# Second half of the sink values loaded in the second batch, the first batch's shifted values copied on VectorE, and a plan with measured first arrivals

## The chip, the cores and the metric

The kernel runs on one core of a Trainium2 chip. The metric is the time of one execution in microseconds (us) on the device, the median of several runs. The engines are TensorE (PE in the profile; PEld are its weight loads), VectorE (DVE), ScalarE (ACT), GpSimd (POOL) and SyncE (SP). POOL issues the large loads of q, k and the weights, SP the loads of v and the stores.

## What is computed

Four batches of attention with 8 heads of 64 over 768 positions, then a mixing layer on the result. Three heads attend to everything before them. The five others ("stream" heads) see the first 4 positions, the sinks, and a window of 64. Cut to what matters:

```python
stream_keep = causal & (is_sink | in_win)        # n_sink = 4, window = 64
a = softmax(where(mask, q @ k.T / 8, -1e9))
x = (a @ v) as [batch, 768, 512]
theta = x @ w_theta
y = w_tok_r @ (x * cos(theta)) + w_tok_i @ (x * sin(theta))
u = x + y
out = u + relu(u @ w_ch)
```

## The kernel before

Every batch goes through the same steps. PE transposes q and k, two heads (a pair) at a time (`turn_qk`, L251), and ACT or DVE copies the result out (`keep_qk`, L258 and L260, tiles `qT`, `kT`). PE multiplies scores into `ps` (L322), ACT takes the exponent into `P` (full heads) or `P_st` (stream heads), POOL cuts `P` at the diagonal (L200) and DVE multiplies `P_st` by the window's mask (L358). `sink_scores` (L385) and `sink_exps` (L389) make the weights of the sinks, `p_sink`. Then `values` (L409) multiplies the weights by v, one row block of 128 positions at a time, `normalize` divides by the sums (L414, L416) into `x`, and `turn_x`, `theta` (L432), `wave` (L437 and L439, `ct` and `st`), `z_real` (L442, DVE) and `z_imag` (L445, POOL, in the first batch partly DVE) prepare the mixing: `mix` (L455, `py`), `make_u` (L459), `channel` (L474) and `finish` (L478). The token weights `wtok` are loaded by POOL (L487), transposed on PE (L494) and copied out by ACT or DVE (L498).

Three copies of v are needed. `vt` holds v in bf16 (`cast_v`, L222). `vx` holds it shifted by 64 positions for the stream heads (`shift_v`: L228 and L229 from `vt` in the first batch, L232 and L233 from the loaded tile later). `vs` holds the sinks' values of all batches: `sink_values` (L244) loads the 4 sink positions of two batches into a small tile `vs_f`, which DVE casts into `vs` (L698). `vs_f` is one buffer, and both halves go through it: batches 0 and 1, then 2 and 3.

In the first batch the loads of v (`load_v`, L218, eight DMAs from SP into the four buffers `st_v`) are held back by a small DVE write that depends on the first transposed k (L216).

All steps are put into a `Plan`. Each has an engine, an estimated duration, the steps that it follows and the buffers that it takes. `Plan.order` runs a list scheduler over these estimates, and the code is emitted in the order of the planned starts. So the estimates set the order of instructions on each engine; what an engine really waits for is set by the data. Buffers also tie engines together: `ps`, `pav` and the theta tiles share two PSUM buffers (pool `s`), the transposes share two others (`x`). The plan's `gate` says when the first loads of q and k arrive, and in it one engine "DMA" carries all transfers, one after the other.

Of the kernel before, what the change touches and what calls it, by code (L numbers as in the profile page):

```python
# [31 lines left out]
class Plan:  # L32
# [3 lines left out]

    LATENCY = {"PE": (230, 0), "ACT": (190, 60), "DVE": (120, 60), "POOL": (150, 60), "SP": (50, 0), "DMA": (2000, 0)}
    SWITCH = {"PE": 95, "ACT": 1300}  # L40
    HOLD = {"PE": 1500, "ACT": 8000}

# [11 lines left out]
    def order(self, free):  # L54
# [26 lines left out]
        while events:  # L81
            now = events[0][0]
            while events and events[0][0] <= now:
                _, _, done = heapq.heappop(events)
                if done is not None:
                    for g in done.give:
                        holding[id(g)] -= 1
                        if holding[id(g)] == 0:
                            slots[g.take] += 1
            for e in engines:  # L90
                if free.get(e, 0) > now:
                    continue
                best = None
                for s in ready.get(e, ()):
                    if ready_at[id(s)] > now or (s.take and slots[s.take] < 1):
                        continue
                    value = -ready_at[id(s)] if e == "DMA" else rank[id(s)] + s.bias
                    if s.mode and s.mode != mode.get(e):
                        value -= self.HOLD.get(e, 0)
                    if best is None or value > best[0]:  # L100
                        best = (value, s)
                if best is None:
                    continue
                s = best[1]
                ready[e].remove(s)
                t = now
                if s.mode and s.mode != mode.get(e):
                    if mode.get(e):
                        t += self.SWITCH.get(e, 0)
                    mode[e] = s.mode  # L110
                if s.take:
                    slots[s.take] -= 1
                s.start, s.end = t, t + s.ns
                out.append(s)
                lat = self.LATENCY[e]
                free[e] = s.end
                heapq.heappush(events, (s.end, count, None))
                heapq.heappush(events, (s.end + lat[0], count + 1, s))
                heapq.heappush(events, (s.end + lat[1], count + 2, None))
                count += 3  # L120
                for n in later[id(s)]:
# [12 lines left out]
def kernel(  # L134
# [14 lines left out]
    nc = tc.nc  # L149
# [393 lines left out]

    cleared = [add(eng, ns, lambda n=n: clear(n)) for n, (eng, ns) in enumerate((("DVE", 900), ("POOL", 1300), ("DVE", 600), ("POOL", 1300)))]
    landed = {}
    gate = [add("DMA", ns, None) for ns in (2600, 2400, 4800)]
    for n in range(4):
        for what in "qk":
            landed[what, 0, n] = gate[min(n, 2)]
# [36 lines left out]
    def v_steps(b):  # L586
        for n in range(4):
            if b == 0:
                issue = add("DVE", 200, lambda n=n: load_v(0, n, kT[n // 2]), [kept["k", 0, n // 2]], take="st_v")
                land = add("DMA", 2000, None, [issue])  # L590
            else:
                issue = add("SP", 1500, lambda b=b, n=n: load_v(b, n), [cast[b - 1, n], xk[b - 1, 5]], take="st_v")
                land = add("DMA", 2000, None, [issue])
            old = [s for key, s in av.items() if key[0] == b - 1] if b else [cleared[1]]
            cast[b, n] = add("DVE" if b == 0 else "POOL", 570 if b == 0 else 830, lambda b=b, n=n: cast_v(nc.gpsimd if b else nc.vector, b, n), [land] + old, give=[issue])
            for x, h in enumerate(PAIRS[n]):
                if not IS_RETR[h]:
                    shift[b, h] = add("POOL", 960, lambda b=b, n=n, x=x: shift_v(nc.gpsimd, b, n, x), [cast[b, n]], give=[issue])

    def attention_steps(b):  # L600
        got = {}
# [56 lines left out]
    def mlp_steps(b):  # L658
        for t in range(NB):
# [6 lines left out]
            ch[b, t] = add("PE", 864, lambda b=b, t=t: channel(b, t), [uk, channel_w], take="m", give=[uk], mode="128")  # L666
            fin = add("DVE", 680, lambda b=b, t=t: finish(b, t), [ch[b, t]], take="ot", give=[ch[b, t], ud[b, t]], bias=URGE)
            st = add("SP", 100, lambda b=b, t=t: store(b, t), [fin])
            add("DMA", 900, None, [st], give=[fin])

    turn_steps(0)
    v_steps(0)
# [19 lines left out]
    weights(4, 2, [])  # L692
    ones_done = add("POOL", 600, sink_ones, [cleared[3]])
    sink_done = []
    for half in range(2):
        first = add("SP", 500, lambda half=half: sink_values(2 * half), [cleared[2]] + sink_done)
        land = add("DMA", 100, None, [first])
        sink_done.append(add("DVE", 480, lambda half=half: nc.vector.tensor_copy(vs[:32, 2 * half:2 * half + 2, :, :D], vs_f), [land, cleared[3], ones_done]))  # L698
# [54 lines left out]
```

## Time and profile before

| what | us |
|---|---|
| median of 3 runs | 226.41 (226.37, 226.41, 229.37) |
| the profiled execution, its own time | 229.25 |
| its span, first to last instruction | 227.5 |
| busy: PE, PEld | 195.2, 113.1 |
| busy: DVE, ACT, POOL | 122.2, 120.2, 101.1 |

The profiled execution is 2.84 us longer than the median, and 1.75 us of its own time lie outside the span. PE is busy for 86% of the span, the other engines for 44% to 54%: the time is that of PE's work and of the places at which PE waits. Times of single instructions below are from the span's start.

### The profile page before, as it was taken

To read this page: it belongs to the slowest core of one execution; us is meant where nothing else is said; L and a number is where in the kernel's file an instruction comes from. 1 tells how busy PE (TensorE), PEld (TensorE's weight loads), DVE (VectorE), ACT (ScalarE), POOL (GpSimd) and SP (SyncE) were. 2 spreads that over 40 slices of the span, in tenths; PEclk is the share of its full clock that TensorE was granted. 3 is DMA by queue.
4 is the path that set the end of the run, shared out by engine and by line. 5 is a ranking of instruction groups with operands and counts; after the bars stand their busy time and mean duration, and the time that the engine had idled before them with its cause. 6 is when DMAs were issued, how large, how long until landed. Compare 5 with 4: busy or idle time off the path is not lost.

```text
span 227.5 us, 5040 instructions
## 1 busy us (share of the span) xinstructions
PE 195.2 (86%) x2124; PEld 113.1 (50%) x2124; DVE 122.2 (54%) x203; ACT 120.2 (53%) x156; POOL 101.1 (44%) x180
## 2 busy tenths in 40 slices
PE   0688549968997899999999999959999999689990
PEld 0555339634554577544553468525544575234440
DVE  6327815389542168479135168495451764974341
ACT  2477402793499960184777563644977526703120
POOL 7955992072488300349852200299835000780000
PEclk9999999999999589999999999997999999999997
DMA  6994599999994934902103000960012000210303
GB/s 76 164 210 108 80 174 213 192 200 199 195 209 98 202 55 118 208 14 81 49 0 127 14 0 3 242 178 0 3 48 94 3 3 0 92 49 0 138 0 140
DMA packets 39759, 22.63 MB, mean 99 GB/s; under 512 B 25912, under 2 KB 36664, under 8 KB 39736
## 3 DMA queue, kind: packets, MB, share of 16 engines
q0 software_dynamic: 11072, 9.70, 27.4%
q1 hardware_dynamic: 28664, 12.61, 21.2%
q8 instruction: 16, 0.26, 0.5%
q14 instruction: 7, 0.06, 0.1%
HBM read 25.71 MB, written 6.29 MB: 141 GB/s over the span
## 4 chain that ended last, share of the span: by engine, by line
PE 72%; DVE 8%; ACT 6%; DMA 5%; POOL 3%; issue 3%; POOLq 1%; SPq 1%; DVEq 0%; ACTq 0%
PE py L455 26%; PE pav L409 9%; PE ps L322 9%; PE pc L474 7%; PE pt L251 7%; PE ps L432 6%; DVE zr L442 5%; POOL zi L445 3%; PE pt L421 3%; PE pt L464 3%; DMA vs_f<-in_v_dram 2%; PE pt L494 2%; DMA kb<-in_k_dram 2%; ACT P L341 2%; ACT P_st L338 1%
## 5 line engine op out<-in xcount | busy, mean ns | idle before, releaser
L455 PE MATMUL py<-zr,wtokTr 128*128 128x512 bf16 x144 | 39.7, 385 | 6.3 <-DVE zr L442 6.3
L445 POOL TENSOR_TENSOR zi<-x,st 128x512 bf16<-128x512 bf16 x20 | 27.8, 1421 | 25.2 <-ACT st L439 19.8
L455 PE MATMUL py<-zi,wtokTi 128*128 128x512 bf16 x144 | 38.5, 379 | 0.1
L459 DVE TENSOR_TENSOR u<-x,py 128x512 bf16<-128x512 bf16 x24 | 16.5, 687 | 36.1 <-PE py L455 36.1
L322 PE MATMUL ps<-qT,kT 64*64 64x128 bf16 (+6 forms) x380 | 26.7, 266 | 6.5 <-ACT P L341 2.2
L442 DVE TENSOR_TENSOR zr<-x,ct 128x512 bf16<-128x512 bf16 x24 | 27.9, 1197 | 1.3 <-ACT ct L437 1.3
L468 ACT COPY uT<-pt 128x512 bf16<-128x512 bf16 x24 | 13.9, 586 | 26.5 <-PE pt L464 26.4
L478 DVE SCALAR_TENSOR_TENSOR ot<-pc,u 128x512 f32<-128x512 f32 x24 | 16.5, 688 | 16.4 <-PE pc L474 15.1
L222 POOL CAST vt<-st_v 128x768 bf16<-128x768 f32 x12 | 10.2, 856 | 33.3 <-DMA st_v<-in_v_dram 33.1
L322 PEld LDWEIGHTS <-kT 64*64 64x64 bf16 (+1 forms) x380 | 13.6, 113 | 21.7 <-issue 17.1
L200 POOL TENSOR_SCALAR_AFFINE_SELECT P<-P 128x256 bf16<-128x256 bf16 (+1 forms) x48 | 16.5, 365 | 17.2 <-ACT P L346 6.6
L474 PE MATMUL pc<-w_ch_sb,uT 128*128 128x512 bf16 x96 | 24.0, 380 | 0.0
L432 PE MATMUL ps<-w_theta_sb,xT 128*128 128x512 bf16 x96 | 23.2, 379 | 0.9 <-ACT st L439 0.9
L437 ACT ACTIVATE ct<-ps,half_pi 128x1024 f32<-128x1024 f32 x12 | 13.0, 1113 | 20.1 <-PE ps L432 19.5
L341 ACT ACTIVATE P<-ps 128x1024 bf16<-128x1024 f32 (+2 forms) x24 | 21.2, 923 | 4.5 <-PE ps L322 4.5
L455 PEld LDWEIGHTS <-wtokTr 128*128 128x128 bf16 x144 | 12.6, 98 | 19.7 <-issue 7.6
L258 ACT COPY qT<-pt 128x768 bf16<-128x768 bf16 x14 | 11.0, 802 | 18.7 <-PE pt L251 18.5
L455 PEld LDWEIGHTS <-wtokTi 128*128 128x128 bf16 x144 | 13.3, 98 | 14.9 <-issue 0.4
L358 DVE TENSOR_TENSOR P_st<-P_st,m_stream 128x512 bf16<-128x512 bf16 (+2 forms) x24 | 12.8, 543 | 14.7 <-ACT P_st L349 10.5
L409 PE MATMUL pav<-vx,P_st 128*128 128x65 bf16 x120 | 17.4, 207 | 3.5 <-POOL vx L228 3.5
L409 PE MATMUL pav<-vt,P 128*128 128x65 bf16 x252 | 16.1, 207 | 1.8 <-DVE x L416 1.8
L409 PE MATMUL pav<-vt,P_st 128*128 128x65 bf16 x120 | 17.5, 208 | 0.0
(73 smaller groups left out, 323.8 us busy)
## 6 DMA issues: line engine op xcount, KB each, us to landing
st_v<-in_v_dram SPq DMA_DIRECT2D x32, 192.0 KB
out_dram<-ot SPq DMA_DIRECT2D x24, 256.0 KB
qb<-in_q_dram POOLq DMA_DIRECT2D x3, 768.0 KB, 10.8
kb<-in_k_dram POOLq DMA_DIRECT2D x3, 768.0 KB, 15.4
wtok<-in_moe_w_tok_r_dram POOLq DMA_DIRECT2D x3, 384.0 KB, 11.9
wtok<-in_moe_w_tok_i_dram POOLq DMA_DIRECT2D x3, 384.0 KB, 12.7
w_theta_sb<-in_moe_w_theta_dram POOLq DMA_DIRECT2D x1, 512.0 KB, 5.7
w_ch_sb<-in_moe_w_ch_dram POOLq DMA_DIRECT2D x1, 512.0 KB, 21.1
```

The source lines that it names most:

```text
L200: nc.gpsimd.affine_select(out=t, in_=t, compare_op=ALU.is_ge, fill=0.0, base=base, pattern=pattern, channel_multiplier=cm)
L251: nc.tensor.transpose(pt[64 * x:64 * x + 64, j * 128:(j + 1) * 128], state[what, b][:, h, j * D:(j + 1) * D], ident)
L322: nc.tensor.matmul(ps[half, yy, c:c + w], l, r, start=True, stop=True, skip_group_check=True)
L341: nc.scalar.activation(P.rearrange("p (y c) -> p y c", y=2), ps[:, :, :w0], AF.Exp, scale=scale)
L409: nc.tensor.matmul(o, l, r, start=(m == 0), stop=True, skip_group_check=True)
L432: nc.tensor.matmul(ps[:, y], state["xT", b][:, kk, (i + y) * 128:(i + y + 1) * 128], w_theta_sb[:, kk], start=(kk == 0), stop=(kk == KD - 1))
L442: nc.vector.tensor_tensor(state["zr", b][:, i + y], state["x", b][:, i + y], state["ct", b, i][:, y], ALU.mult)
L445: (nc.vector if eng == "DVE" else nc.gpsimd).tensor_tensor(state["zi", b][:, i + y], state["x", b][:, i + y], state["st", b, i][:, y], ALU ...
L455: nc.tensor.matmul(py, wtokT[n][:, s, t * 128:(t + 1) * 128], z[:, s], start=(g == 0 and m == 0), stop=(g == 2 and m == 3))
L459: nc.vector.tensor_tensor(u, state["x", b][:, t], state.pop(("py", b, t)), ALU.add)
L474: nc.tensor.matmul(pc, uT[:, kk], w_ch_sb[:, kk], start=(kk == 0), stop=(kk == KD - 1))
L478: nc.vector.scalar_tensor_tensor(ot, state.pop(("pc", b, t)), 0.0, state.pop(("u", b, t)), ALU.max, ALU.add)
```

## The change

Three parts. The second half of the sink values (`sink_values(2)` and its cast) moves from the first batch into the second (`sink_steps(1, ...)`, after `v_steps(1)`). In the first batch the shifted copies `vx` are made on DVE, not on POOL. And the plan's estimates change: the first arrivals in `gate`, the time of a v load's issue on SP, and a second planned transfer engine "DMAH" for the DMAs that SP issues. The estimates alter no instruction, but the whole order is planned anew from them, in all four batches.

```diff
-    gate = [add("DMA", ns, None) for ns in (2600, 2400, 4800)]
+    gate = [add("DMA", ns, None) for ns in (4300, 2000, 6000)]
...
-                land = add("DMA", 2000, None, [issue])
+                land = add("DMAH", 2000, None, [issue])
             else:
-                issue = add("SP", 1500, lambda b=b, n=n: load_v(b, n), [cast[b - 1, n], xk[b - 1, 5]], take="st_v")
-                land = add("DMA", 2000, None, [issue])
+                issue = add("SP", 700, lambda b=b, n=n: load_v(b, n), [cast[b - 1, n], xk[b - 1, 5]], take="st_v")
+                land = add("DMAH", 2000, None, [issue])
...
-                    shift[b, h] = add("POOL", 960, lambda b=b, n=n, x=x: shift_v(nc.gpsimd, b, n, x), [cast[b, n]], give=[issue])
+                    shift[b, h] = add("POOL" if b else "DVE", 960 if b else 340, lambda b=b, n=n, x=x: shift_v(nc.gpsimd if b else nc.vector, b, n, x), [cast[b, n]], give=[issue])
...
-            add("DMA", 900, None, [st], give=[fin])
+            add("DMAH", 900, None, [st], give=[fin])
...
-    for half in range(2):
-        first = add("SP", 500, lambda half=half: sink_values(2 * half), [cleared[2]] + sink_done)
-        land = add("DMA", 100, None, [first])
-        sink_done.append(add("DVE", 480, lambda half=half: nc.vector.tensor_copy(vs[:32, 2 * half:2 * half + 2, :, :D], vs_f), [land, cleared[3], ones_done]))
+    def sink_steps(half, after):
+        first = add("SP", 1500, lambda: sink_values(2 * half), [cleared[2]] + after)
+        land = add("DMAH", 300, None, [first])
+        sink_done.append(add("DVE", 480, lambda: nc.vector.tensor_copy(vs[:32, 2 * half:2 * half + 2, :, :D], vs_f), [land, cleared[3], ones_done]))
+
+    sink_steps(0, [])
     attention_steps(0)
     for b in range(1, B):
         turn_steps(b)
         v_steps(b)
+        if b == 1:
+            sink_steps(1, [sink_done[0], cast[1, 0]])
```

The order on DVE in the first batch, from the loads of v to the first row of values: before, from the second cast of v to the division of row 0 (L414, L416).

```order
L222 CAST vt<-st_v 128x2x6x64
L358 TENSOR_TENSOR P_st<-P_st,m_stream 128x2x8x64
L222 CAST vt<-st_v 128x2x6x64
L358 TENSOR_TENSOR P_st<-P_st,m_stream 128x2x8x64
L358 TENSOR_TENSOR P_st<-P_st,m_stream 128x8x64
L698 CAST vs<-vs_f 32x10x64
L222 CAST vt<-st_v 128x2x6x64
L358 TENSOR_TENSOR P_st<-P_st,m_stream 128x2x4x64 x2
L358 TENSOR_TENSOR P_st<-P_st,m_stream 128x4x64
L698 CAST vs<-vs_f 32x10x64
L414 RECIPROCAL r<-pav 128x8
L416 TENSOR_TENSOR x<-pav,r 128x2x4x64
```

The second `L698` stands directly ahead of the first division. The same engine in the changed kernel, from the first cast of v (it follows the two copies `kT_92` and `kT_93` of the first two pairs):

```order
L222 CAST vt<-st_v 128x2x6x64
L698 CAST vs<-vs_f 32x10x64
L228 COPY vx<-vt 64x390
L229 COPY vx<-vt 64x325
L358 TENSOR_TENSOR P_st<-P_st,m_stream 128x8x64
L222 CAST vt<-st_v 128x2x6x64
L260 COPY qT_90<-pt 128x768
L260 COPY kT_94<-pt 128x768
L222 CAST vt<-st_v 128x2x6x64
L260 COPY qT_91<-pt 128x768
L260 COPY kT_95<-pt 128x768
L222 CAST vt<-st_v 128x2x6x64
```

The first cast of v, the one remaining sink cast and the first shifted copy now stand ahead of the copies of the third and fourth pair (`qT_90` to `kT_95`), which they followed before. From there to the first division:

```order
L358 TENSOR_TENSOR P_st<-P_st,m_stream 128x2x8x64
L228 COPY vx<-vt 64x390
L229 COPY vx<-vt 64x325
L228 COPY vx<-vt 64x390
L229 COPY vx<-vt 64x325
L358 TENSOR_TENSOR P_st<-P_st,m_stream 128x2x8x64
L228 COPY vx<-vt 64x390
L229 COPY vx<-vt 64x325
L228 COPY vx<-vt 64x390
L229 COPY vx<-vt 64x325
L358 TENSOR_TENSOR P_st<-P_st,m_stream 128x2x4x64 x2
L358 TENSOR_TENSOR P_st<-P_st,m_stream 128x4x64
```

Four more shifted copies stand between the masks, and no sink cast is left ahead of the division, which follows. On SP, before:

```order
L244 DMA vs_f<-in_v_dram 4x2x64 x5
L218 DMA st_v<-in_v_dram 128x6x64 x8
L244 DMA vs_f<-in_v_dram 4x2x64 x5
L218 DMA st_v<-in_v_dram 128x6x64 x8
L481 DMA out_dram<-ot 128x512 x3
```

And in the changed kernel:

```order
L244 DMA vs_f<-in_v_dram 4x2x64 x5
L218 DMA st_v<-in_v_dram 128x6x64 x16
L244 DMA vs_f<-in_v_dram 4x2x64 x5
L481 DMA out_dram<-ot 128x512 x3
L218 DMA st_v<-in_v_dram 128x6x64 x8
```

The second batch's eight v loads moved ahead of the second sink load. On POOL, at the end of the first batch and the start of the second, before:

```order
L487 DMA wtok<-in_moe_w_tok_r_dram 128x2x768
L487 DMA wtok<-in_moe_w_tok_i_dram 128x2x768
L208 DMA qb<-in_q_dram 128x8x384
L445 TENSOR_TENSOR zi<-x,st 128x512 x2
L208 DMA kb<-in_k_dram 128x8x384
L240 COPY kS_97<-kT_94 64x4 x2
L240 COPY kS_98<-kT_95 64x4 x2
L222 CAST vt<-st_v 128x2x6x64
L232 CAST vx<-st_v 64x6x64
L233 CAST vx<-st_v 64x5x64
```

And in the changed kernel:

```order
L487 DMA wtok<-in_moe_w_tok_r_dram 128x2x768
L445 TENSOR_TENSOR zi<-x,st 128x512 x2
L222 CAST vt<-st_v 128x2x6x64
L487 DMA wtok<-in_moe_w_tok_i_dram 128x2x768
L222 CAST vt<-st_v 128x2x6x64 x2
L232 CAST vx<-st_v 64x6x64
L233 CAST vx<-st_v 64x5x64
L232 CAST vx<-st_v 64x6x64
L233 CAST vx<-st_v 64x5x64
L232 CAST vx<-st_v 64x6x64
L233 CAST vx<-st_v 64x5x64
L240 COPY kS_97<-kT_94 64x4 x2
```

The second batch's casts of v now follow the two `zi` at once, ahead of the small sink keys `kS`; the loads of q and k for the third batch come later. On DVE at that place the order before is one `L498`, four `zr` (L442), one `L498`, two `zi`, two `zr`, two `zi`; in the changed kernel it is four `zr`, two `zi`, two `L498`, two `zr`, two `zi`. On PE the row blocks of values in the first batch came in the order 0, 5, 2, 1, 4, 3 and come now in the order 0, 2, 1, 4, 5, 3; the six transposes of a token weight that stood among them (L494) now stand behind the first products with `w_theta`.

More of the change, by code (lines that the diff above doesn't have):

```diff
@@ L32 @@
 class Plan:
-    LATENCY = {"PE": (230, 0), "ACT": (190, 60), "DVE": (120, 60), "POOL": (150, 60), "SP": (50, 0), "DMA": (2000, 0)}
+    LATENCY = {"PE": (230, 0), "ACT": (190, 60), "DVE": (120, 60), "POOL": (150, 60), "SP": (50, 0), "DMA": (2000, 0), "DMAH": (2000, 0)}
     SWITCH = {"PE": 95, "ACT": 1300}
@@ L96, in order @@
                         continue
-                    value = -ready_at[id(s)] if e == "DMA" else rank[id(s)] + s.bias
+                    value = -ready_at[id(s)] if e[:3] == "DMA" else rank[id(s)] + s.bias
                     if s.mode and s.mode != mode.get(e):
```

## The prediction

> **What bounds the kernel now.** I read the busy shares first, then PE's own waits, then the chain of work that ended last, then the timelines of the first 60 us. PE is busy for 86% of the span, so time is won where PE waits. Of PE's waits (us in total, times, longest) one stands in this change's reach by itself:
>
> ```profile
> PE pav L409 <- POOL vx L228: 3.5, 3, 1.5
> ```
>
> The first batch's value rows wait 3.5 us for POOL's shifted copies. The chain (start, us, what) shows what comes behind:
>
> ```profile
> 25.71 0.68 DVE vs L698
> 27.75 5.37 DMA vs_f<-in_v_dram
> 33.19 0.51 DVE vs L698
> 33.85 0.70 DVE x L416
> 34.60 1.50 PE pav L409 x24
> 36.10 0.43 PE pt L421 x4
> 36.52 0.64 PE pt L494 x6
> 37.16 2.81 PE pav L409 x51
> 39.97 0.72 PE pt L421 x8
> 40.69 0.84 PE pav L409 x27
> 41.76 0.86 PE ps L432 x4
> ```
>
> `vs_f` is one tile, so its second load follows the first cast. DVE takes its work in order and waits for that load with the division behind it, and the third value row, which needs a `ps` buffer back, starts only at 34.60. The reader is also to see a pace: 51 value products take 2.81 us (55 ns each) up to 39.97, 27 take 0.84 (31 ns) after it. PE runs at half pace until it has worked without a break for about 5.8 us from 34.60, to 40.4.
>
> **First part: the start of the first batch.** The changed order puts the first cast of v ahead of DVE's copies of pairs 2 and 3, so the arrival of v is a new wait, and with it come late `qT` and `kT`, for which PE's scores wait. Of the eight pieces of 192 KB that SP asks for, the hardware queue had moved from 8 us on, up to 16, to 20 and to 21.5 us (packets, MB, share):
>
> ```profile
> q1 hardware_dynamic: 2755, 0.69, 38.8%
> q1 hardware_dynamic: 5859, 1.47, 54.7%
> q1 hardware_dynamic: 6272, 1.57, 52.0%
> st_v<-in_v_dram SPq DMA_DIRECT2D x32, 192.0 KB
> ```
>
> That is 3.6, 7.7 and all eight pieces. They are asked for in order, so I take the first pair's two as there by 16.0, the second's soon after and the third's by 20. The prices on DVE, what DVE did at 16, and what POOL gives up:
>
> ```profile
> L260 DVE COPY kT<-pt 128x768 bf16<-128x768 bf16 x10 | 9.2, 949 | 4.5 <-PE pt L251 4.5
> L358 DVE TENSOR_TENSOR P_st<-P_st,m_stream 128x1024 bf16<-128x1024 bf16 x8 | 6.3, 783 | 3.8 <-ACT P_st L338 3.6
> L358 DVE TENSOR_TENSOR P_st<-P_st,m_stream 128x512 bf16<-128x512 bf16 x12 | 5.2, 443 | 0.9 <-ACT P_st L349 0.5 <-ACT P_st L338 0.4
> ...
> L222 DVE CAST vt<-st_v 128x768 bf16<-128x768 f32 x4 | 2.6, 639 | 0.0
> ...
> L228 POOL COPY vx<-vt 64x390 bf16<-64x390 bf16 x5 | 3.1, 619 | 1.6 <-DVE vt L222 1.5
> ```
>
> ```profile
> 15.96 0.96 DVE L260 COPY qT<-pt 128x768 bf16<-128x768 bf16 x1 [4.05 <-PE pt L251]
> 33.63 0.18 DVE L414 RECIPROCAL r<-pav 128x8 f32<-128x8 f32 x1
> ```
>
> DVE was idle for 4.05 us before 15.96, so the wait to 16.0 costs nothing; what stands between it and `qT` does. No row shows a shifted copy on DVE. Above stands twice POOL's 0.62 for the larger of the two pieces, 1.2 us; below, half of what DVE's cast gives for 390 + 325 of its 768 elements (0.639 x 715 / 768 = 0.59), since it reads half the bytes: 0.3. I take 0.5 for both, nearest to DVE's own cast.
>
> From 16.0 DVE then does a cast 0.64, the sink cast 0.6 (between its 0.68 and 0.51), `vx` 0.5, a mask 0.44 and a cast 0.64: 18.8. Then `qT` and `kT` (0.95 each): 20.7; a cast, `qT`, `kT`: 23.3. What PE did at these points before:
>
> ```profile
> 20.52 0.85 PE L322 MATMUL ps<-qT,kT 64*64 64x128 bf16 x26
> 22.29 0.92 PE L322 MATMUL ps<-qT,kT 64*64 64x128 bf16 x26 [0.92 <-ACT P_st L338]
> 24.06 0.40 PE L322 MATMUL ps<-qT,kT 64*128 64x256 bf16 x2 [0.85 <-ACT P_st L338]
> 24.55 1.76 PE L385 MATMUL ps<-qT,kS 128*128 128x512 bf16 x6
> ```
>
> PE reached pair 2 at 20.52 by its own work, so 20.7 costs 0.2. Pair 3 waits for 23.3, 1.0 later. The two products at 24.06 with their 0.85 of waiting now stand earlier in the order, so the sink scores start about 0.35 later than 24.55 and end at 26.7. On DVE a cast, a mask of 0.78, two `vx`, a mask of 0.78 and two `vx` follow 23.3 and end at 27.5; then the last shifted copy is there, and row 0 is done at 27.8. Row 2 takes 24 x 0.055 = 1.3, to 29.1. Three small masks (0.44, 0.44 and under that) end at about 28.75, the division (0.18 + 0.70) at 29.65, a buffer is free, and the third value row starts at 29.7 against 34.60: 4.9 earlier.
>
> From there PE has four rows of 21 + 30 + 33 + 27 = 111 products and 16 transposes (0.43, 0.43, 0.72) before theta: at half pace 6.2 + 1.6 = 7.75, to 37.45. If full pace comes 5.8 us after 29.7 again, at 35.5, the last 1.95 shrink by half and theta starts at 36.5, where before it started at 41.6 (a little ahead of the chain's 41.76). **Term: -5.1 us.** Its bounds are -4.1 (half pace throughout) and -6.3 (the first rival). The loads keep up: on SP the second batch's v is asked for right behind the first's, and on POOL, rid of `vx`, `w_theta` and the token weights come earlier too.
>
> **Second part: theta to the first mixing.** This stage hangs on theta and moves with it, but its order changed on DVE, POOL and ACT (the last two rows are ACT's and PE's):
>
> ```profile
> 46.84 5.39 DVE L442 TENSOR_TENSOR zr<-x,ct 128x512 bf16<-128x512 bf16 x4
> 52.62 1.28 DVE L445 TENSOR_TENSOR zi<-x,st 128x512 bf16<-128x512 bf16 x2
> 48.64 3.59 DVE L442 TENSOR_TENSOR zr<-x,ct 128x512 bf16<-128x512 bf16 x1
> 49.38 2.29 POOL L445 TENSOR_TENSOR zi<-x,st 128x512 bf16<-128x512 bf16 x2
> 147.98 4.21 DVE L442 TENSOR_TENSOR zr<-x,ct 128x512 bf16<-128x512 bf16 x3
> 49.09 0.82 ACT L498 COPY wtokTr<-pt 128x768 bf16<-128x768 bf16 x1
> 52.28 2.10 PE py L455 x9
> ```
>
> A `zr` or `zi` takes DVE 0.64 (half of 1.28) when POOL is idle. The fourth `zr` took 3.59: it ended after both of POOL's `zi` were through. A load issue that stood ahead of those `zi` on POOL is gone, so the fourth `zr` may now pass first: up to 2.9 won on DVE. But POOL casts the second batch's v right behind its two `zi`, so the six `zi` and `zr` that ran alone before run beside it. Where POOL was busy throughout, three `zr` took 4.21, 1.4 each or 0.75 more than alone: 6 x 0.75 = 4.5 lost. PE's own limit is that the transposes of the imaginary token weight now wait for two ACT copies behind `st` (49.09 and 2 x 0.82, then two transposes of 0.2 to 0.25): `py` starts at 51.2 or later in this stage's old time, 1.1 ahead of 52.28 at best. Worse than taking turns is that one of DVE's waits spans POOL's whole queue:
>
> ```profile
> L222 POOL CAST vt<-st_v 128x768 bf16<-128x768 f32 x12 | 10.2, 856 | 33.3 <-DMA st_v<-in_v_dram 33.1
> L232 POOL CAST vx<-st_v 64x384 bf16<-64x384 f32 x15 | 8.0, 534 | 0.4
> L233 POOL CAST vx<-st_v 64x320 bf16<-64x320 f32 x15 | 7.2, 480 | 0.7
> ```
>
> Three casts and six shifted pieces are 3 x 0.86 + 3 x 1.01 = 5.6. The ends are thus -1.1 and 5.6 - 2.9 = +2.7; taking turns gives 4.5 - 2.9 = +1.6. I take **+0.5**, between the better end and taking turns, which a row shows.
>
> The rule of the Trainium skill (SBUF — State Buffer, "Who interferes with whom") is that a DVE instruction with two SBUF inputs and a POOL instruction that reads SBUF exclude each other for one whole instruction. By it each of the six waits for one POOL instruction at most, and the term ends at taking turns, +1.6. The 3.59 row agrees that they exclude each other, but its wait spanned two, so I leave the end at +2.7.
>
> **The rest.** The second sink cast costs 0.51 on DVE, now behind the third `u`. It lies where DVE had nothing to do, up to the third `u`'s row and after it:
>
> ```profile
> 63.33 0.69 DVE L459 TENSOR_TENSOR u<-x,py 128x512 bf16<-128x512 bf16 x1 [3.59 <-PE py L455]
> ```
>
> Without that cover it would cost its 0.5. Its five small DMAs stand on SP behind the v loads and ahead of the first store, and nothing waits for them in the first batch. The new estimates also reorder batches 2 and 3; the same instructions run there, I can read no gain or loss from their order, and take 0 with 1.5 to either side.
>
> **Sum.** -5.1 + 0.5 = -4.6 us. The terms come from the profiled execution of 229.25 us (span 227.5), 2.84 longer than the median of 226.41; they lie in stages that every execution has, so I take them from the median: 226.4 - 4.6 = 221.8 us.
>
> **Rivals.** First, more is won: full pace comes 3.4 us after 29.7, at 33.1, theta starts at 35.3 (-6.3), and the stage's better end adds -1.1: 219.0. For it: 5.8 us is a single observation. Against it: it is the only one. The Trainium skill (TensorE: Matmul & The Clock Gate, "What's actually happening") states that a free-running window of 3.4 us, once busy, opens PE's clock; by that rule the opening lies between 33.1 and 36.5 here, -6.3 to -4.6. The trace's 5.8 us agree with it.
>
> Second, DVE bounds the first 30 us: a pair's shifted copy costs 1.2 us as on POOL. The five are 3.5 more, and so is theta's start: -1.6 + 0.5, 225.3. For it: POOL's selects and load issues run beside these copies. Against it: a cast of twice the bytes takes DVE 0.64.
>
> Third, the gain is handed back later. In the second batch ACT's exponents are the limit (length, then busy us of PE, PEld, DVE, ACT, POOL):
>
> ```profile
> 71.10:74.50 3.40, 1.73 (x17) 0.87 (x15) 1.12 (x2) 3.27 (x6) 2.91 (x7) 1.00 0.62 72
> ```
>
> ACT works 3.27 of 3.40 us there, PE 1.73. If the new order lengthens this or a later stretch by what was won, the time is 226.4. Against it: ACT starts there once PE has transposed, which comes earlier.
>
> Fourth, slower: v comes late. If the eight pieces advance together and not in order, the first pair is there only at 21.5, with all. DVE, whose queue it heads, stands until then, and everything in the first part comes 5.5 us later: +0.4 + 0.5, 227.3. It decides from an arrival at 20.6 on (16.0 + 4.6). For it: the first cast ran after 20 before, so no row shows an earlier arrival. Against it: the pieces were asked for one behind the other.
>
> **Chances and numbers.** The forecast of 221.8 has 0.46 (220 to 223.5), the first rival 0.24, the second 0.16, the third 0.10, the fourth 0.04. The range of 218.5 to 225.8 holds the forecast and nearly all of the first and second rivals, and leaves out 0.2: the third, the fourth and the edges. A measurement of this kernel can tell about 2%, 4.5 us, from no change: the limit is 221.9. Faster by more holds the first rival and half the forecast, 0.47; slower by more would need the fourth rival and as much again lost in the reordered batches, 0.03; within 2% is the rest, 0.50.
>
> **What would show it.** Right: no wait of DVE for `vs_f`; PE's waits for `vx` under 1 us; the third value row near 29.7, theta near 36.5, and `py` some 4.6 us before 52.28. Wrong: pair 2's scores well after 20.7 (v late), a shifted copy of 0.5 or more on DVE, a DVE `zr` or `zi` over 2 us in the first batch, or a lead at 60 us that is gone at 104 or 146.

## The result and the profile after

The changed kernel takes 220.75 us, the median of four runs (220.08 to 221.44), beside 227.82 us of the kernel before in the same measurement (226.37 to 229.37). The ratio is 0.969, 95% interval 0.959 to 0.978: faster. A second measurement, shown with the experiments, gave 221.03 us and a ratio of 0.982, interval 0.975 to 0.989. All ratios compare only the executions within 1.5% of a kernel's fastest, and since the kernel before spreads from 222.9 to 230.7 us in the measurements of the experiments, only 13 of its 31, 11 of 29, 2 of 17 and 3 of 11 executions count there, so that the medians of all runs lie further apart than the ratios say.

The profiled execution took 220.35 us, its span is 218.6 (227.5 before). Of the waits that carried the prediction none of PE for `vx` and none of DVE for `vs_f` is left. The table of PE's waits (us in total, times, longest) has these two instead among its first:

```profile
PE py L455 <- DVE zr L442: 3.2, 3, 1.2
PE ps L432 <- ACT st L439: 2.6, 1, 2.6
```

The chain of waits (start, us, what) at the place where the kernel before stood still until 34.60:

```profile
25.36 0.58 PE ps L385
25.95 0.22 issue
26.17 0.96 PE ps L385 x4
...
27.22 0.70 ACT p_sink L389
...
27.97 1.49 PE pav L409 x24
...
29.47 1.05 PE pav L409 x21
30.52 0.22 PE pt L421 x4
30.74 0.93 PE pav L409 x30
31.67 0.22 PE pt L421 x4
31.89 1.82 PE pav L409 x58
```

The third value row starts at 29.47. The reader should divide: 24 products in 1.49 us are 62 ns each, 30 in 0.93 and 58 in 1.82 are 31 ns each. Full pace comes inside the row of 29.47; the clock's first record stands at 30.04. Before, it was 40.4.

Where the lead comes from and goes to, as starts of PE's (and once DVE's) first such row in the two profiled executions:

| point | before | after | lead |
|---|---|---|---|
| first batch's theta (L432) | 41.59 | 34.69 | 6.9 |
| first `u` on DVE (L459) | 57.99 | 52.87 | 5.1 |
| first channel product (L474) | 64.91 | 59.77 | 5.1 |
| second batch's theta | 91.09 | 84.73 | 6.4 |
| last batch's first transposes (L251) | 146.71 | 140.73 | 6.0 |
| last batch's theta | 188.18 | 179.57 | 8.6 |
| end of the span | 227.54 | 218.65 | 8.9 |

So the start won 6.9, the stage from theta to the first `u` gave 1.8 back, and later stretches won 3.8 more. The last number is in good part a matter of the clock, as far as two profiles can tell. The clock's records stand on a grid of 3.413 us; before, three windows of it with work on PE (74.55 and 77.96, 153.06) were at half pace after the first opening, in the changed kernel one. The view by windows of the changed kernel (length, then busy us of PE, PEld, DVE, ACT, POOL, then PE's clock), the exponents' stretch of the second batch:

```profile
67.59:71.00 3.41, 1.62 (x14) 0.79 (x12) 1.83 (x3) 3.41 (x6) 2.36 (x6) 1.00 1.28 224
71.00:74.41 3.41, 3.41 (x56) 2.96 (x56) 1.06 (x4) 3.35 (x6) 1.08 (x3) 0.50 1.25 235
```

ACT is full in the first, PE works 1.62 of 3.41 us; the next window is at half pace, though PE now has work throughout.

### The profile page after: what moved, and what is told of

It reads as the page before. It is cut to its first block, busy times and chain, and to the rows that moved or that the text cites. A ratio compares the mean times of both kernels' runs of the same rounds, so it can differ in the third digit from the quotient of the medians.

```text
span 218.6 us, 5007 instructions
## 1 busy us (share of the span) xinstructions
PE 188.4 (86%) x2094; PEld 109.1 (50%) x2124; DVE 124.7 (57%) x213; ACT 119.5 (55%) x156; POOL 100.0 (46%) x170
## 4 chain that ended last, share of the span: by engine, by line
PE 69%; DVE 8%; ACT 7%; DMA 5%; issue 4%; POOL 4%; SPq 1%; POOLq 1%; DVEq 0%; ACTq 0%
PE py L455 25%; PE pav L409 9%; PE pc L474 8%; PE ps L322 7%; PE ps L432 6%; PE pt L251 5%; POOL zi L445 3%; PE pt L464 3%; PE pt L421 3%; DVE kT L260 2%; DMA st_v<-in_v_dram 2%; DMA kb<-in_k_dram 2%; PE ps L385 2%; DVE zr L442 2%; ACT ct L437 1%
## 5 line engine op out<-in xcount | busy, mean ns | idle before, releaser
L455 PE MATMUL py<-zr,wtokTr 128*128 128x512 bf16 x129 | 36.2, 379 | 4.6 <-DVE zr L442 3.2
L459 DVE TENSOR_TENSOR u<-x,py 128x512 bf16<-128x512 bf16 x24 | 16.5, 686 | 34.6 <-PE py L455 34.5
L322 PE MATMUL ps<-qT,kT 64*64 64x128 bf16 (+5 forms) x380 | 26.4, 265 | 6.0 <-ACT P L341 2.3
L442 DVE TENSOR_TENSOR zr<-x,ct 128x512 bf16<-128x512 bf16 x24 | 24.8, 1072 | 6.3 <-ACT ct L437 6.3
L200 POOL TENSOR_SCALAR_AFFINE_SELECT P<-P 128x256 bf16<-128x256 bf16 (+1 forms) x48 | 17.7, 397 | 19.0 <-ACT P L344 11.1
L432 PE MATMUL ps<-w_theta_sb,xT 128*128 128x512 bf16 x92 | 23.1, 379 | 2.8 <-ACT st L439 2.6
L474 PE MATMUL pc<-w_ch_sb,uT 128*128 128x512 bf16 x90 | 23.2, 380 | 0.3
L338 ACT ACTIVATE P_st<-ps 128x1024 bf16<-128x1024 f32 (+1 forms) x16 | 12.7, 810 | 8.9 <-PE ps L322 8.8
L416 DVE TENSOR_TENSOR x<-pav,r 128x512 bf16<-128x512 f32 x24 | 16.6, 692 | 0.8
L358 DVE TENSOR_TENSOR P_st<-P_st,m_stream 128x512 bf16<-128x512 bf16 (+2 forms) x24 | 12.1, 515 | 7.9 <-ACT P_st L349 5.8
L409 PE MATMUL pav<-vx,P_st 128*128 128x65 bf16 x120 | 16.1, 202 | 0.5 <-issue 0.5
L409 PE MATMUL pav<-vt,P_st 128*128 128x65 bf16 x120 | 16.1, 202 | 0.0
```

The source lines that it names most:

```text
L200: nc.gpsimd.affine_select(out=t, in_=t, compare_op=ALU.is_ge, fill=0.0, base=base, pattern=pattern, channel_multiplier=cm)
L322: nc.tensor.matmul(ps[half, yy, c:c + w], l, r, start=True, stop=True, skip_group_check=True)
L409: nc.tensor.matmul(o, l, r, start=(m == 0), stop=True, skip_group_check=True)
L416: nc.vector.tensor_tensor(dst, av[:, :, :, :D], r.unsqueeze(3).to_broadcast([128, 2, 4, D]), ALU.mult)
L432: nc.tensor.matmul(ps[:, y], state["xT", b][:, kk, (i + y) * 128:(i + y + 1) * 128], w_theta_sb[:, kk], start=(kk == 0), stop=(kk == KD - 1))
L442: nc.vector.tensor_tensor(state["zr", b][:, i + y], state["x", b][:, i + y], state["ct", b, i][:, y], ALU.mult)
```

## The experiments

Twelve kernels were timed, two of them for a second time, in four measurements, each beside the kernel before on the same chip. Medians are of all runs; "ratio" below is that of the table.

| kernel | median (lowest to highest, runs) | before, median | ratio, 95% interval |
|---|---|---|---|
| sink move alone | 226.58 (224.10 to 228.68, 10) | 228.59 | 1.000 [0.995, 1.006] |
| copies on DVE alone | 226.07 (224.33 to 227.65, 10) | 228.59 | 1.002 [0.995, 1.008] |
| estimates alone | 223.82 (222.12 to 225.62, 10) | 228.59 | 0.990 [0.985, 0.995] |
| changed, copies back on POOL in the same order | 226.09 (225.00 to 226.82, 10) | 228.59 | 1.000 [0.995, 1.005] |
| changed again | 221.03 (219.76 to 222.51, 6) | 228.32 | 0.982 [0.975, 0.989] |
| estimates alone, again | 224.07 (223.01 to 226.31, 12) | 228.32 | 0.996 [0.991, 1.000] |
| estimates and sink move | 223.64 (222.23 to 225.57, 12) | 228.32 | 0.991 [0.986, 0.996] |
| both edits, old estimates | 225.12 (223.00 to 226.28, 12) | 228.32 | 1.000 [0.996, 1.005] |
| two of PE's waits filled | 221.09 (220.69 to 221.77, 6) | 228.67 | 0.985 [0.976, 0.994] |
| casts of v behind the z | 223.27 (220.97 to 223.82, 12) | 228.67 | 0.993 [0.984, 1.002] |
| products of zeros at the start | 220.76 (219.22 to 221.46, 6) | 228.67 | 0.983 [0.972, 0.993] |
| casts of v truly held | 222.46 (220.11 to 222.89, 6) | 228.20 | 0.987 [0.977, 0.997] |

**The sink move alone.** The loop over the halves becomes the changed kernel's `sink_steps`, with the old estimates.

```diff
-    for half in range(2):
-        first = add("SP", 500, lambda half=half: sink_values(2 * half), [cleared[2]] + sink_done)
+    def sink_steps(half, after):
+        first = add("SP", 500, lambda: sink_values(2 * half), [cleared[2]] + after)
...
+        if b == 1:
+            sink_steps(1, [sink_done[0], cast[1, 0]])
```

> The kernel before, with the second sink load and its cast moved into the second batch and nothing else; in the first batch only one cast leaves DVE's queue. Theory (two things each delayed the third value row): without the 5.37 us wait for vs_f the division follows row 0, which PE ends at 31.0 because it still waits 3.5 us for vx on POOL; the third value row starts near 32.0 instead of 34.60, the break of 1.80 us before it shrinks below 0.8, and full PE clock comes one step of 3.41 us earlier (37.0 instead of 40.42). Theta starts near 38 (41.6 before): 223.0 us, ratio 0.985. Rival (the waits for vx alone bound this stage): third value row within 0.5 us of 34.6 and no gain, 226.4.

In its profile DVE no longer waits for `vs_f`; it waits for PE, and PE waits for `vx` as long as ever (3.5 us in three waits). The chain shows POOL's order behind it, with a load issue of 0.96 us between two pairs' copies:

```profile
23.13 0.75 POOL vx L228
...
23.93 0.55 POOL vx L229
24.47 0.96 POOL wtok L487
...
25.48 0.84 POOL vx L228
...
29.17 3.22 PE pav L409 x59
```

Behind that the value rows run on without a break, and the first batch's theta starts at 36.03, 30.0 us after PE's first instruction (35.1 in the profile before). So the wait was a real one there. The measured ratio shows no gain all the same: this profile is the fastest of ten executions (224.10), and the other nine took 225.8 to 228.7. By the medians of all runs this kernel is 2.0 us below the kernel before, which the ratio doesn't confirm. Nor need the 5 us of theta all be due to the edit: in this execution the clock was open from 11.6 to 15.0, in the profile before not until 40.42. The expected 223.0 was a miss.

**The copies on DVE alone.** The one line of `shift[b, h]` in the diff of the change, with the old estimates.

> The kernel before, with the first batch's shifted copies on DVE and its planner told so; the planner also puts the second sink cast behind the zr of the first batch. Theory: PE's three waits for vx (3.5 us) go, and the wait for vs_f falls into a place where DVE has time; the casts of v still stand behind the copies of pairs 2 and 3. Third value row near 31, theta near 37.5: 222.5 us, ratio 0.982. Rival (DVE bounds the first 30 us and takes 1.2 us for a pair's shifted copy): the row starts near 34 and the time is 226.

PE's waits for `vx` are now for DVE, 2.7 us in four, since the copies stand at the end of DVE's work behind late casts of v. A miss too: 226.07, ratio 1.002, the time of the rival but not by its mechanism. In the profile (224.33) the third value row starts at 28.51 and theta at 34.80, earlier than the theory had them, with the clock open from 12.4 to 26.1. This execution, too, is the fastest of its ten.

**The estimates alone.** `gate`, "DMAH", 700 ns for SP's load of v and the new planned times of the sink loads, with copies on POOL and both sink loads in the first batch.

> The kernel before with the planner's new estimates alone (first arrivals, own queue for the hardware DMAs, 700 ns for a load of v): shifted copies stay on POOL, both sink loads stay in the first batch. Theory (the gain is made by the two removed waits, the estimates only put the casts of v earlier): DVE still waits for vs_f and PE for vx, third value row at 33 to 35, 225.5 us, ratio 0.996. Rival (the order is what wins, and the two edits are incidental): 222 us or less, ratio 0.98.

Theory and rival were both off. The new order alone takes one wait away: the second sink cast is no longer waited for, it stands at 27.74 among DVE's work and follows the masks at once (timeline of DVE: start, us, what):

```profile
26.02 1.80 DVE L358 TENSOR_TENSOR P_st<-P_st,m_stream 128x1024 bf16<-128x1024 bf16 x3 [0.74 <-ACT P_st L338]
27.74 0.83 DVE L698 CAST vs<-vs_f 32x640 bf16<-32x640 f32 x1
28.58 0.21 DVE L414 RECIPROCAL r<-pav 128x8 f32<-128x8 f32 x1
```

The first cast of v comes at 15.34 in place of about 20, so the first sink cast is early, the second load is early, and the copies on POOL can be early too. Here PE waited for none of them; in the run that repeats this kernel it did, for 1.1 us in two waits.

**The changed kernel with the copies back on POOL, in the same order.** Only the engine of `shift_v` in the first batch differs.

```diff
-lambda b=b, n=n, x=x: shift_v(nc.gpsimd if b else nc.vector, b, n, x)
+lambda b=b, n=n, x=x: shift_v(nc.gpsimd, b, n, x)
```

> The changed kernel in its own order on every engine, with the ten shifted copies of the first batch run by POOL in place of DVE. Theory: POOL does them behind its load issues, at 1.2 us a pair, so the last is there near 31 and not at 27.6; row 0 waits for it, a break of over 1 us falls into the value rows, and full clock comes 3.41 us later too: theta 3 to 4 us later, 224 us (about 1.5% over the changed kernel). Rival (POOL has time there and the place of the copies is indifferent): within 0.5 us of the changed kernel, 220.7.

As the theory had it, only larger: the last copy ends at 31.6 (27.6 in the changed kernel), PE waits 3.5 us for `vx`, the clock opens at 36.68 (30.04), theta starts at 38.73 (34.69), and in the ratio the whole gain is gone.

```profile
PE pav L409 <- POOL vx L228: 3.5, 3, 1.6
```

**The parts beside each other.** One measurement of the changed kernel, the estimates alone, the estimates with the sink move (copies planned and run on POOL again), and both edits with the old estimates.

> The changed kernel itself, timed beside its parts. Theory (the grid of 3.413 us windows on which PE's clock is granted lies otherwise against the program in each execution, and a window at half pace costs 1.2 to 1.7 us): times fall into groups that far apart between 220 and 224 us, median 221.5, 3% under the kernel before. Rival (the change takes the clock's steps away as it takes the waits away): all within 220.1 to 221.4 as in the first four runs.

> The kernel before with the planner's new estimates alone, again, now beside the changed kernel. Theory E (the estimates alone remove both waits, since POOL's copies and the second sink cast are then ordered early enough; the two edits add nothing): the same median as the changed kernel within 1 us. Theory A (the edits are worth the 3 us by which this kernel stood behind the changed kernel in other executions): 1.5 to 3 us above it.

> The changed kernel with the first batch's shifted copies planned and run on POOL again; estimates and sink move kept. Theory E: POOL has time for the copies where the planner now puts them, ahead of the load issues, and DVE is 2.9 us freer: the same as the changed kernel within 1 us. Theory A (the copies on DVE are needed): PE waits for vx on POOL again, 1 us or more in sum, and the time is 1.5 to 3 us above the changed kernel.

> The changed kernel with the planner's old estimates: sink move and copies on DVE kept. Theory E: the casts of v stand behind the copies of pairs 2 and 3 again, PE waits for vx about 2.7 us in sum as with the copies moved alone, and little more is won than with either edit alone: 225.5 to 226.5. Theory A (the two removed waits are the gain): the changed kernel's time within 1 us.

Neither of the two theories in these expectations stands as a whole. Theory A's numbers came for the estimates alone (3.0 us above the changed kernel) and for the estimates with the sink move (1.6 us of waits, 2.6 above), but the edits without the estimates, which by A should reach the changed kernel, stay 4.1 above it; that is near E's number (225.12 for 225.5 to 226.5). In the ratio the edits without the estimates bring nothing (1.000; by the medians 3.2 us, which the ratio doesn't confirm), the estimates alone 0.4 to 1%, and all together 1.8%. Adding the sink move to the estimates moves the median by 0.4 us, inside the spread; adding the copies on DVE to those two moves it by 2.6. What the copies on DVE take away is PE's wait for POOL, in the profile of estimates and sink move

```profile
PE pav L409 <- POOL vx L228: 1.6, 2, 0.8
```

and its consequence for the clock: in that execution it opens 28.0 us after PE's first instruction and theta starts 30.3 us after it; in the two of the changed kernel it opens after 23.2 to 23.3 and theta starts after 27.9 and 28.0. This is not the whole difference. In the first profile of the estimates alone PE waits for no `vx` and theta starts after 27.5 us, and from PE's first instruction to the end of the span the execution is 1.2 us longer than the changed kernel's all the same (213.1 beside 211.9), with three windows at half pace behind the opening in place of one. Not run were the changed kernel without its sink move, so that what the move adds is not shown, and the estimates one by one.

The changed kernel's six times fall into 219.8 to 220.2 with a mean granted clock of 0.990, and 221.9 to 222.5 with 0.966 to 0.972: two groups 2 us apart, about as the theory on the clock's grid expected. What a grid can do is seen at PE's wait of 2.62 us for ACT ahead of the third pair of theta rows, which the changed kernel and nearly all the others have (0.9 us in the kernel before and in the sink move alone). First the changed kernel in its second profile, then estimates and sink move (columns as above):

```profile
39.86:43.28 3.42, 1.50 (x7) 0.68 (x7) 3.09 (x5) 3.42 (x5) 1.71 (x2) 1.00 1.29 199
43.28:46.69 3.41, 3.33 (x25) 1.88 (x24) 3.41 (x5) 2.70 (x4) 3.41 (x4) 1.00 1.17 208
```

```profile
40.80:44.22 3.42, 0.80 (x7) 0.39 (x5) 2.50 (x4) 3.42 (x4) 1.25 (x2) 1.00 1.22 207
44.22:47.63 3.41, 3.41 (x18) 1.92 (x16) 3.08 (x3) 2.54 (x4) 3.41 (x3) 0.50 1.20 208
```

It is the same wait. In one execution an edge of the grid cuts it, and the window has 1.5 us of PE's work; in the other it lies in one window whole, 0.80 us of work are left, and the next window runs at half pace: 18 instructions where the other had 25.

**Two waits filled.** The test of that: products of zeros into an unused bank where PE waits.

```diff
+            if b == 0 and i == 4:
+                pw = ps_m.tile([128, DM], F32, tag="m", name="pw")
+                for _ in range(10):
+                    nc.tensor.matmul(pw, warm[:, :128], warm, start=True, stop=True)
...
+        if b == 3 and t == 0 and g == 0:
+            for _ in range(5):
+                nc.tensor.matmul(py, warm[:, :128], warm, start=True, stop=True)
```

> The changed kernel with products of zeros into an unused bank on PE: ten of 128x512 ahead of the first batch's third pair of theta rows, where PE waits 2.62 us for ACT, and five ahead of the last batch's first mixing product, where it waits 1.23 and 1.19 us for zr. At full pace ten are 2.2 us and five 1.1 us, so they end before what PE waits for; no other work moves. Theory (a window of the clock's grid with about 2 us or more of PE's waits in it puts the next window at half pace, 1.2 to 1.7 us lost, and where the grid lies decides in which executions): the upper group of the changed kernel's times (221.9 to 222.5, granted clock under 0.975) goes, median 220.0, all within 1 us. Rival (the groups come from something else, arrivals of data for one): two groups as before, median 221 or, where the products stand in the way, 221.5 or more.

The groups went: all six executions have a clock of 0.978 to 0.991 and lie within 1.1 us. That fits the clock as the cause of the upper group. But the lower group went too (the fastest is 220.69, beside 219.76), and the median did not fall (221.09 beside 221.03): half a miss, and what sets the groups apart is not shown by it alone. The one profile shows the rest of PE's wait at theta (0.46 us), so the products did not stand in the way there, and two windows at half pace in the exponents' stretch (68.37 to 75.19) where the changed kernel's profiles have one. Whether that is this execution's grid or a cost of the products was not settled.

**Casts of v behind the z.** The stage that gave 1.8 us back. In the changed kernel POOL casts the second batch's v beside DVE's `zr` and `zi`; here these casts are put behind them in the order.

```diff
+    early = [s for s in order[:last] if s in cast_1]
+    order = [s for s in order[:last + 1] if s not in early] + early + order[last + 1:]
```

> The changed kernel with the second batch's casts of v on POOL held until DVE has done the last zi of the first batch; no other row moves. Theory (DVE and POOL take turns, so DVE's zr and zi take 1.2 to 1.4 us beside POOL's casts and 0.64 alone): the four zr and zi behind POOL's own two zi take 0.64 each, DVE reaches the copies of kT some 2 us earlier, PE's waits of 0.53, 0.49 and 0.29 us near 50 us shrink, the lead at the first transposes of u is 1.0 to 1.5 us larger: 220.0. Rival (PE is behind DVE only by those short waits, and POOL's later casts are covered): 220.7, the changed kernel's time within 0.5 us.

This tested nothing: moved behind one load issue on POOL, whose order knows nothing of DVE, the casts still started at 46.19, beside the same `zr`. It did give one row: a `zr` of 2.66 us, over POOL's three casts back to back (2.37 us). The median, 223.27, is some 2 us above the changed kernel's; why is open.

**Products of zeros at the start.** Twelve on PE ahead of the first keys.

```diff
+    pw = ps_m.tile([128, DM], F32, tag="m", name="pw")
+    for _ in range(12):
+        nc.tensor.matmul(pw, warm[:, :128], warm, start=True, stop=True)
```

> The changed kernel with twelve products of zeros (128x512) on PE at its start, while it waits for the first keys (6.4 to 6.8 us); nothing else moves. Theory (a window without waits opens the clock, and the scores that follow, with under 1.6 us of waits in a window, keep it open): full pace from about 7 to 10 us on, the score products and transposes of the first batch take half, value rows start at full pace: theta 1.5 to 2.5 us earlier, 219. Rival (the short products of the scores don't hold the clock open, or DVE, ACT and the arrival of v set that stage's end and not PE): the clock closes again before 20 us, 221.0.

The clock opened at 6.72 and closed at 13.55, behind windows with 1.3 and 1.55 us of waits between short score products. Theta came 27.1 us after the first keys' transposes (27.9 and 28.0), and the time is the changed kernel's (220.76). The rival holds.

**Casts of v truly held.** As two runs before, with a copy of one column of the last `zi` on POOL ahead of the casts.

```diff
+    def after_z(fn=first.fn):
+        nc.gpsimd.tensor_copy(held, state["zi", 0][:, 5, :1])
+        fn()
```

> As the run before with the casts of v behind the zi, but held there in truth: ahead of them POOL copies one column of the last zi of the first batch, so it waits until DVE has written it; the imaginary token weights' load stands ahead of that wait. Theory (the first batch's zr and zi are slow on DVE because POOL casts v beside them): the two zr and two zi behind POOL's own zi take 0.64 us each (1.23 and 0.98 to 1.30 in the changed kernel), the first u of the first batch comes 1.2 to 1.9 us earlier against the start of theta, PE's waits for zi (0.82 us in sum) go. POOL's work for the second batch comes 3 to 4 us later, and sink scores, which need its key copies, may give up to 1 us back: 220.0 to 221.0, beside 221.0 of the changed kernel. Rival (these instructions are slow for another reason): zr and zi stay over 0.95 us and the first u where it was, 221.5 or more.

DVE's timeline, first of the changed kernel, then of this one:

```profile
40.11 2.50 DVE L442 TENSOR_TENSOR zr<-x,ct 128x512 bf16<-128x512 bf16 x4 [4.73 <-ACT ct L437]
42.94 2.81 DVE L445 TENSOR_TENSOR zi<-x,st 128x512 bf16<-128x512 bf16 x2 [0.34 <-ACT st L439]
45.67 1.01 DVE L498 COPY wtokTi<-pt 128x768 bf16<-128x768 bf16 x2
46.61 2.47 DVE L442 TENSOR_TENSOR zr<-x,ct 128x512 bf16<-128x512 bf16 x2
49.00 2.21 DVE L445 TENSOR_TENSOR zi<-x,st 128x512 bf16<-128x512 bf16 x2
```

```profile
40.18 2.50 DVE L442 TENSOR_TENSOR zr<-x,ct 128x512 bf16<-128x512 bf16 x4 [4.73 <-ACT ct L437]
43.01 2.80 DVE L445 TENSOR_TENSOR zi<-x,st 128x512 bf16<-128x512 bf16 x2 [0.34 <-ACT st L439]
45.87 1.02 DVE L498 COPY wtokTi<-pt 128x768 bf16<-128x768 bf16 x2
46.81 1.28 DVE L442 TENSOR_TENSOR zr<-x,ct 128x512 bf16<-128x512 bf16 x2
48.01 1.29 DVE L445 TENSOR_TENSOR zi<-x,st 128x512 bf16<-128x512 bf16 x2
50.52 1.82 DVE L260 COPY kT<-pt 128x768 bf16<-128x768 bf16 x2 [1.23 <-PE pt L251]
```

With POOL held, two `zr` and two `zi` take 0.64 us each, and PE waits for no `zi`. The two `zi` beside POOL's own are as slow as ever. So the cause of the slow `zr` and `zi` is shown. The time did not gain: DVE was at the copies of `kT` early and waited 1.23 us for PE, whose clock was at half pace in this execution from 41.77 to 45.18, behind the wait of 2.62 us. Against theta the first `u` came 17.5 us later (18.2 in the changed kernel); five of six executions had a mean clock under 0.975, and the median is 222.46, a miss.

None of these kernels beats the changed one by more than its spread.

## Why the prediction came out

**The time, 221.8 us against 220.75, and the range** held. The sum was -4.6 from a median of 226.4; the two medians of the result are 7.1 apart. That the time came within 1.1 us is in part luck. Between the two profiled executions the three terms are -6.9, +1.8 and -3.8, or -8.9 in sum, each off by more than 1 us; two of the misses have one sign and one the other, and the forecast started 2.84 us below the execution from which its terms were read.

**First part, start of the batch: the waits right, the clock's part of the term mis-sized, -5.1 predicted and -6.9 in the profiles.** v's first pair was there in time, as forecast (first cast at 15.79 for 16.0). DVE's walk fits row by row: the third `kT` ended at 20.5 for 20.7, the fourth at 22.9 for 23.3, the last shifted copy at 27.57 for 27.5. The third value row started at 29.47 for 29.7. A pair's copy, forecast at 0.5 between 0.3 and 1.2, took 0.65 in the mean:

```profile
L229 DVE COPY vx<-vt 64x325 bf16<-64x325 bf16 x5 | 1.6, 329 | 0.1
L228 DVE COPY vx<-vt 64x390 bf16<-64x390 bf16 x5 | 1.6, 323 | 0.0
```

That is above the 0.5 which the prediction named as a sign of being wrong; it did no harm, since DVE's walk as a whole ended in time.

What failed is the sentence "If full pace comes 5.8 us after 29.7 again, at 35.5". It came at 30.04. The 5.8 us were counted from the third row because a break of 1.80 us stood ahead of that row before. They were the rest of the grid's window that held the break and one full window, as the view of the kernel before shows:

```profile
33.59:37.00 3.41, 2.40 (x35) 2.41 (x36) 2.55 (x7) 0.44 (x1) 1.96 (x3) 1.00 1.23 228
37.00:40.42 3.42, 3.42 (x60) 3.42 (x59) 1.34 (x5) 0.95 (x2) 0.00 (x0) 1.00 1.28 193
```

In the changed kernel no break stands there, PE works from 26.17 on almost without waits, and the grid's window from 26.63 to 30.04 is full but for 0.15 us (the clock column reads 1.00 ahead of 40.42 above and ahead of 30.04 here because the traces have no record ahead of their first):

```profile
26.63:30.04 3.41, 3.26 (x52) 2.98 (x51) 3.19 (x10) 0.69 (x1) 1.65 (x3) 1.00 1.18 199
30.04:33.45 3.41, 3.41 (x107) 3.41 (x105) 2.62 (x7) 1.17 (x2) 0.00 (x0) 1.00 1.19 199
```

Twice as many instructions fit into the second. From the third row to theta it then took 5.2 us and not 6.8. That the break was a cause of the late clock and not only its own length was not in the sum. The first rival had the same fault: it counted 3.4 us from 29.7 too. For this part its -6.3 came nearer than the forecast's -5.1, but its other half, a gain of 1.1 in the next stage, did not come. The rule of the Trainium skill (TensorE: Matmul & The Clock Gate, "What's actually happening"), that the window is free-running and does not start with the work, is what the traces show: all records of an execution lie 3.413 us or a multiple apart. By that rule the opening here lies between one and two windows after 26.17, at 29.6 to 33.0 (an estimate), and the trace's 30.04 does.

**Second part, theta to the mixing: +0.5 predicted, +1.8 measured up to the first `u`.** The fourth `zr` did pass first (four in 2.50 us, 5.39 before), so the 2.9 us were won. At the prediction's own mark, `py` at 52.28, nothing was lost yet: that row began with the fourth product, which came at about 45.3 in the changed kernel (an estimate, from the first product at 44.68 and 0.215 us for each), 6.9 earlier. The loss lies behind it, where PE waits for `zi` (0.29 and 0.53 us) and for DVE's copy of `kT` (0.49), and shows at the first `u`. The three slow rows of the changed kernel's timeline above cost 2.81 + 2.47 + 2.21 - 6 x 0.64 = 3.65 us, where taking turns was put at 4.5; a weight's copy moved into this place (0.5), a wait of 0.34 for `st` and 0.2 ahead of the first `zr` make up the +1.8. The step that failed is "I take +0.5, between the better end and taking turns". The end that a row showed, +1.6, was the better value, though in part by luck: the slow rows cost 0.85 less than it had, and the weight's copy and the two waits, which it did not have, 1.04 more. The rule of the Trainium skill (SBUF — State Buffer, "Who interferes with whom") led to that end too; the held casts agree with the rule, 0.64 us alone and 1.1 to 1.4 in the mean of a row beside POOL. A `zr` of 2.66 us over three POOL instructions shows again that a wait can span more than the one instruction.

**Third part.** The second sink cast (0.83 us at 58.80) lay behind the third `u`, as forecast; it is followed by 1.2 us of DVE's idleness.

**Batches 2 to 4: "0 with 1.5 to either side", measured 3.8 won from the first channel product on.** This lies outside the stated bounds. In the profiles two windows fewer at half pace, worth up to 1.7 us each, and 1.7 us less of waits for `zr` near 150 us would cover it. That would be the grid and the new order together; how much is whose is not shown, and in other executions the windows lie elsewhere.

**The rivals.** The second (copies at POOL's price) and the fourth (v late) did not happen. The third, that the gain is handed back later, did not either; a small part of it went into the new wait of 2.62 us for ACT, which the prediction did not name as the next one (the third pair of theta rows starts 6.3 us earlier, the first 6.9). That neither edit gains in the ratio without the estimates, and that the estimates alone gain 0.4 to 1%, was not among the rivals at all: the prediction took the order as given and costed the two waits.

**What stays open.** Why the sink move alone and the copies on DVE alone, in whose profiles theta starts 5.1 and 6.5 us sooner after PE's first instruction than in the kernel before, gain nothing in the ratio. Both profiles are the fastest of ten executions, the times of the first kernel spread over 4.6 us, and one trace per kernel doesn't tell where the other executions lost it.

## What to carry to other kernels

A planner's estimate can be an edit in its own right: with first arrivals as measured, casts and copies moved ahead of the work that had hidden them, and only on top of that did the edits that remove a wait show a gain in the ratio here. A wait of PE is worth up to its own length and, where it leaves half a window of the clock's grid or more empty, often up to half of the next window too (1.7 us); so find out which waits lie close together, and time a kernel over many executions, since the grid lies otherwise in each. Work moved to an idle engine is not free if it slows the busy one, as POOL's casts did to DVE's `zr` and `zi` (0.64 us alone, 1.1 to 1.4 beside them): hold it by a true dependency, since a place in another engine's order holds nothing.

## What was unexpected of the hardware

The size of the spread: the kernel before took 222.9 to 230.7 us over 88 runs, the changed one 219.8 to 222.5 in the second measurement, on one core and with mean granted clocks from 0.92 to 0.99. A part of it is the arrival of the first keys: PE's first transpose stands at 6.0 to 7.7 us in the profiles. The limit for a step down is not one number in the traces: 1.85 us without PE's work in a window left the clock up in one place (197.43 before) and 1.92 in another (39.86 in the second profile of the changed kernel), and 2.0 to 2.6 brought it down in others, but among the short score products 1.3 to 1.8 were often enough. Nor did full work of that kind always open it: before 20 us, windows with 0.0 to 0.3 us of waits left it at half pace in the profiles of the kernel before and of the changed one, while in the profiles of both edits and of the sink move alone one such window did open it, at 12.0 and 11.6, for 3.4 us, and in that of the copies on DVE alone one with 0.5 us, at 12.4, for 13.7 us. What decides over the clock in a window was not settled.
